# Where VectorE's transform pieces, token combinations and output transpositions stand between two matmul products

## The chip, the cores and the metric

The kernel runs on one core of one Trainium2 chip. The metric is device time in microseconds (us) of one execution. On one core no run can be checked against a second core; the timed runs of both kernels were all classed as fast, and the runs of one kernel agree within 0.3%. One part that varies is the start-up before the first step, 124 to 128 us in the profiled runs. Differences below that are read from the trace of one profiled execution, where a step has a length that repeats to 0.01 us.

## The reference, cut to what matters

```python
# batch, seq, dim = 8, 3008, 256;  d_ff = 2048
X = np.fft.rfft(x, axis=1)                       # along the sequence
y = np.fft.irfft(X * (filt_r + 1j * filt_i), n=seq, axis=1)
h = y.reshape(24064, 256) @ w_in                 # 256 -> 2048
return (h * sigmoid(h)) @ w_out                  # 2048 -> 256
```

The Fourier part is done by matmuls with small tables (stage 1, forward, inverse, stage 3), with additions and multiplications on VectorE between them. The two large products are done by a Strassen-like scheme with seven products in place of eight, which costs extra additions on VectorE.

## The kernel before

All of the time after the start-up is one sequence of 384 steps: 8 batches of 48. A step computes one eighth of the hidden layer of a "pair" (two blocks of 256 or 240 token columns each) and projects the previous step's result. Eight steps make a pair, six pairs a batch. While batch b goes through its 48 steps, the pieces of the transform of batch b+1 are slipped between them. In the timelines VectorE's instructions start in program order (in step 30 the transpositions at 995.67, the token combinations at 996.36, the products at 997.85 and only then the addition behind them at 999.05), so the *place* of a piece in the program decides what it delays.

A step has eight rounds. What VectorE must do in it (lines with `combine(v, ...)`), and when, is set here:

```python
def hidden(step):                                   # ... = cuts
    mm(xo, A11, yt[:, 0, 0:n], True)                # round 0
    nc.scalar.copy(out=sums[:, 0, 0:n], in_=xo)
    yield
    mm(zo, A12, yt[:, 1, 0:n], True)                # round 1
    combine(v, g[:, 0, 0:n], zo, sums[:, 0, 0:n], ALU.add)      # first g<-pyz
    finish()                                        # two g<-g of the step before
    yield
    ...
    mm(yo, S1, t[:, 0, 0:n], True)                  # round 3
    yield
    mm(xo, S3, t[:, 1, 0:n], False)                 # round 4
    nc.scalar.copy(out=sums[:, 2, 0:n], in_=xo)
    combine(v, g[:, 2, 0:n], yo, sums[:, 2, 0:n], ALU.add)      # middle g<-pyz
    ...
    mm(yo, S4, yt[:, 1, n:2 * n], False)            # round 7: overwrites what the middle one read
    combine(v, g[:, 1, 0:n], yo, sums[:, 1, 0:n], ALU.add)      # last g<-pyz
    silu(1)
    combine(v, g[:, 4:6, 0:n], g[:, 1:3, 0:n], g[:, 0:2, 0:n], ALU.subtract)
```

`yo` and `zo` are the two halves of the PSUM tile `pyz`, of which there is one buffer. So product S4 (round 7) waits for the middle addition, and the next step's A12 (round 1) waits for the last one: where they are late, S4 starts 0.47 us after the start of the middle addition (999.05 and 999.52 us, step 30 of the kernel before), A12 0.46 us after that of the last one (935.67 and 936.13 us, behind step 22 of the changed kernel).

The pieces that share VectorE with these, with their times from one start to the next as worked out below:

```python
def multiply(g, k):      # two products of 128x512 out of PSUM: 1.20 us
def add(g, k):           # two sums of 128x256: 0.67 us
def rows(g, i, n=2):     # two sums of 128x512 out of PSUM, then DMAs to d2: 1.32 us
def tokens(pair):        # ty: one 128x512 and two 128x256 differences: 1.49 us
def output(pair, chunk): # two transpositions of 128x256, then 8 DMAs out: 0.69 us
```

Places are given as (step, round); `put` queues a piece, and after each round all that is due is emitted:

```python
def put(step, rnd, piece, *args):
    pending.append((step + rnd / ROUNDS, len(pending), lambda: piece(*args)))
...
for g, step in enumerate((-38, -35, -29, -27, -22, -19)):
    put(at + step, 3, part["forward"], g)
    put(at + step, 5, part["multiply"], g, 0)
    put(at + step + 1, 1, part["multiply"], g, 1)
    put(at + step + 1, 5, part["add"], g, 0)
    put(at + step + 2, 1, part["add"], g, 1)
...
for rnd in range(ROUNDS):
    work = [w for w in work if next(w, work) is not work]   # hidden(step), project(step - 1)
    until(step + rnd / ROUNDS)                              # the pieces due
```

A piece with round 1 to 3 comes to stand behind the first addition and `finish` and ahead of the middle addition: I call this the step's *first interval*. A piece with round 4 to 6 comes between the middle and the last addition: the *second interval*.

## Time and profile before

| | before |
|---|---|
| time, median of 3 (lowest to highest) | 2706.57 us (2706.18 to 2706.76) |
| TensorE busy, weight loads busy | 96%, 80% of the span |
| VectorE, ScalarE, GpSimd busy | 62%, 41%, 17% |
| from the first to the last instruction | 2705.5 us |
| of this ahead of step 0 | 126.6 us |
| one batch of 48 steps (third batch) | 323.1 us |

The table of windows, for the third batch alone (columns: window, its length, then busy time of TensorE, weight loads, VectorE, ScalarE, GpSimd, the granted TensorE clock, DMA share and rate):

```profile
785.40:1108.40 323.00, 320.34 (x2305) 267.91 (x2304) 202.26 (x435) 134.73 (x371) 48.23 (x72) 1.00 0.24 59
```

The granted clock is 1.00 and the DMA share 0.24 in this window, so neither limits the batch as a whole (one step, 36, does wait for a load; it is taken up below). TensorE is shown idle for 2.66 us in the 323 us. The prediction explains why that is only about half of what is lost.

### The profile page before, as it was taken

To read this page: it belongs to the slowest core of one execution; us is meant where nothing else is said; L and a number is where in the kernel's file an instruction comes from. 1 tells how busy PE (TensorE), PEld (TensorE's weight loads), DVE (VectorE), ACT (ScalarE), POOL (GpSimd) and SP (SyncE) were. 2 spreads that over 40 slices of the span, in tenths; PEclk is the share of its full clock that TensorE was granted. 3 is DMA by queue.
4 is the path that set the end of the run, shared out by engine and by line. 5 is a ranking of instruction groups with operands and counts; after the bars stand their busy time and mean duration, and the time that the engine had idled before them with its cause. 6 is when DMAs were issued, how large, how long until landed. Compare 5 with 4: busy or idle time off the path is not lost.

```text
span 2705.5 us, 47315 instructions
## 1 busy us (share of the span) xinstructions
PE 2600.5 (96%) x18432; PEld 2162.2 (80%) x18432; DVE 1675.9 (62%) x3554; ACT 1100.6 (41%) x3000; POOL 448.3 (17%) x653
## 2 busy tenths in 40 slices
PE   4589999999999999999999999999999999999998
PEld 1368888788887888878887888878888788888987
DVE  4886665666566665666656666566665666555554
ACT  1244344443444344444344434444344443444443
POOL 3542111211111111111101111021111111100100
PEclk9599999999999999999999999999999999999999
DMA  9633121421223202331123212132122421110000
GB/s 210 188 101 76 43 49 38 108 61 30 47 66 98 54 24 52 81 86 40 43 53 78 69 56 49 38 98 58 40 49 50 107 53 31 42 34 20 9 16 16
DMA packets 203616, 166.26 MB, mean 61 GB/s; under 512 B 120896, under 2 KB 175808, under 8 KB 203264
## 3 DMA queue, kind: packets, MB, share of 16 engines
q1 hardware_dynamic: 184728, 111.11, 18.3%
q0 software_dynamic: 14992, 47.46, 5.8%
q10 hardware_dynamic: 3672, 4.67, 0.7%
q8 instruction: 145, 2.38, 0.4%
q14 instruction: 79, 0.65, 0.1%
HBM read 88.17 MB, written 74.97 MB: 60 GB/s over the span
## 4 chain that ended last, share of the span: by engine, by line
PE 84%; DVE 9%; DMA 3%; SPq 1%; ACT 1%; issue 1%; POOL 0%; DVEq 0%; ACTq 0%
PE acc L538 37%; PE px L479 22%; PE pyz L479 17%; DVE g L450 3%; PE pd L391 3%; PE pa L292 2%; PE pb L315 2%; PE pc L348 2%; DMA t<-d 1%; DVE q L367 1%; DVE ty L450 1%; DVE p L327 1%; DVE o L568 1%; DVE z L327 1%; DMA x<-in_x_dram 1%
## 5 line engine op out<-in xcount | busy, mean ns | idle before, releaser
L538 PE MATMUL acc<-g,w_t 128*128 128x256 f32 (+1 forms) x5376 | 1513.3, 375 | 0.4 <-DVE g L450 0.4
L538 PEld LDWEIGHTS acc<-g,w_t 128*128 128x128 f32 x5376 | 1022.2, 190 | 116.0 <-DVE g L450 0.8
L450 DVE TENSOR_TENSOR g<-pyz,abc 128x256 f32<-128x256 f32 (+1 forms) x1152 | 478.7, 416 | 590.2 <-ACT abc L500 351.3
L450 DVE TENSOR_TENSOR g<-g 128x256 f32<-128x256 f32 (+3 forms) x1152 | 617.3, 536 | 196.7 <-ACT g L483 183.5
L479 PE MATMUL px<-ty,w_t 128*128 128x256 f32 (+1 forms) x2304 | 690.7, 381 | 4.1 <-ACT abc L494 3.5
L483 ACT ACTIVATE g<-g 128x256 f32<-128x256 f32 (+1 forms) x1152 | 473.3, 411 | 265.6 <-DVE g L450 265.5
L450 POOL TENSOR_TENSOR s<-s 128x256 f32<-128x256 f32 (+1 forms) x329 | 259.2, 805 | 1596.7 <-DVE s L556 1515.2
L479 PEld LDWEIGHTS px<-ty,w_t 128*128 128x128 f32 x2304 | 422.5, 190 | 118.1 <-issue 58.0
L479 PE MATMUL pyz<-y,w_t 128*128 128x256 f32 (+1 forms) x1536 | 461.9, 382 | 18.7 <-DVE g L450 16.9
L479 PEld LDWEIGHTS pyz<-y,w_t 128*128 128x128 f32 x1536 | 278.6, 190 | 83.0 <-DVE g L450 46.7
L494 ACT COPY abc<-px 128x256 f32<-128x256 f32 (+1 forms) x384 | 141.4, 368 | 369.1 <-PE px L479 369.1
L483 ACT ACTIVATE g<-px 128x256 f32<-128x256 f32 (+1 forms) x384 | 146.0, 380 | 300.0 <-PE px L479 300.0
L500 ACT COPY abc<-px 128x256 f32<-128x256 f32 (+1 forms) x384 | 143.2, 373 | 304.8 <-PE px L479 304.6
L479 PE MATMUL px<-y,w_t 128*128 128x256 f32 (+1 forms) x768 | 228.5, 379 | 3.6 <-ACT g L483 2.7
L479 PE MATMUL pyz<-ty,w_t 128*128 128x256 f32 (+1 forms) x768 | 225.4, 375 | 0.7 <-DVE g L450 0.7
L479 PEld LDWEIGHTS px<-y,w_t 128*128 128x128 f32 x768 | 143.1, 190 | 29.2 <-issue 11.1
L479 PEld LDWEIGHTS pyz<-ty,w_t 128*128 128x128 f32 x768 | 145.6, 190 | 18.3 <-DVE g L450 1.8
L487 ACT COPY abc<-px 128x256 f32<-128x256 f32 (+1 forms) x384 | 134.7, 351 | 2.7 <-PE px L479 1.3
L213 DVE COPY y<-pd 128x376 f32<-128x376 f32 x64 | 51.3, 807 | 107.0 <-PE pd L391 107.0
L297 POOL DMA_DIRECT2D d<-t x124 | 64.7, 526 | 294.4 <-ACT abc L500 278.0
L391 PEld LDWEIGHTS pd<-wi_t,t 48*64 48x64 f32 x4096 | 70.7, 140 | 37.6 <-issue 21.9
L315 PE MATMUL pb<-t,d_t 64*32 64x256 f32 x1536 | 62.2, 411 | 38.2 <-DMA t<-d 37.2
(52 smaller groups left out, 1283.8 us busy)
## 6 DMA issues: line engine op xcount, KB each, us to landing
t<-d SPq DMA_DIRECT2D x96, 256.0 KB, 3.9
t<-d SPq DMA_DIRECT2D x128, 192.0 KB, 3.7
d<-t POOLq DMA_DIRECT2D x124, 192.0 KB, 3.0
d<-q POOLq DMA_DIRECT2D x85, 256.0 KB, 2.6
out_dram<-o SPq DMA_DIRECT2D x636, 32.0 KB, 1.8
x<-in_x_dram SPq DMA_DIRECT2D x120, 128.0 KB, 2.9
x<-in_x_dram SPq DMA_DIRECT2D x120, 60.0 KB, 2.8
raw<-in_moe_w_in_dram SPq DMA_DIRECT2D x16, 256.0 KB, 5.9
```

The lines of the kernel that those rows point to most:

```text
L292: nc.tensor.matmul(out=ps[h][64 * par:64 * par + 64], lhsT=wf_t[rows, par], rhs=ut[rows, par], start=True, stop=True)
L297: nc.gpsimd.dma_start(out=d1[par].rearrange("s p n c -> (s p) n c")[:, 4 * u:4 * u + 4, :], in_=t1[64 * par:64 * par + 2 * NS].rearrange(" ...
L315: nc.tensor.matmul(out=ps[k][32 * j:32 * j + 32, ri, :], lhsT=d_t[rows, 4 * g + at, ri, :], rhs=t2[rows, at, :], start=True, stop=True)
L327: nc.vector.tensor_tensor(out=dst, in0=banks[g][k], in1=f_t[m][:, g, k:k + 1, :].to_broadcast([128, 2, C]), op=ALU.mult)
L391: nc.tensor.matmul(out=ps[h][c0:c0 + 64, cb, i, :], lhsT=t4s[g][rows, i, 128 * cb + c0:128 * cb + c0 + 64], rhs=wi_t[rows, :], start=True, ...
L450: eng.tensor_tensor(out=out, in0=in0, in1=in1, op=op)
L479: nc.tensor.matmul(out=out, lhsT=w_t[:, c, 0, jp], rhs=rhs, start=start, stop=True, skip_group_check=True)
L483: nc.scalar.activation(out=g[:, k, 0:n], in_=g[:, k, 0:n] if src is None else src, func=AFT.Silu)
L487: nc.scalar.copy(out=sums[:, 0, 0:n], in_=xo)
L494: nc.scalar.copy(out=sums[:, 1, 0:n], in_=xo)
L500: nc.scalar.copy(out=sums[:, 2, 0:n], in_=xo)
L538: nc.tensor.matmul(out=acc[pair][i][:, h, 0:n], lhsT=w_t[:, c, 1, jp], rhs=g[:, k, 0:n], start=(jp == 0 and h == 0), stop=last, skip_group ...
```

## The change

Its intent: VectorE has room for a piece in each of the two intervals of a step, so each interval should get one large piece or two small ones, in place of two or three large ones in one interval and none in the next. No instruction is added or removed.

```diff
-        for g, step in enumerate((-38, -35, -29, -27, -22, -19)):
-            put(at + step, 3, part["forward"], g)
-            put(at + step, 5, part["multiply"], g, 0)
-            put(at + step + 1, 1, part["multiply"], g, 1)
-            put(at + step + 1, 5, part["add"], g, 0)
-            put(at + step + 2, 1, part["add"], g, 1)
+        for g, places in enumerate((
+                ((-38, 3), (-37, 3), (-37, 5), (-36, 3), (-36, 5)),
+                ((-35, 3), (-35, 5), (-34, 3), (-33, 2), (-33, 5)),
+                ((-29, 3), (-29, 5), (-28, 3), (-28, 5), (-27, 2)),
+                ((-27, 3), (-27, 5), (-26, 3), (-25, 3), (-24, 3)),
+                ((-22, 5), (-21, 3), (-21, 5), (-20, 2), (-20, 5)),
+                ((-20, 3), (-19, 3), (-19, 5), (-18, 3), (-18, 5)))):
+            pieces = (("forward", g), ("multiply", g, 0), ("multiply", g, 1), ("add", g, 0), ("add", g, 1))
+            for (step, rnd), (piece, *args) in zip(places, pieces):
+                put(at + step, rnd, part[piece], *args)
         for g, step in ((0, -32), (2, -24), (4, -16)):
             put(at + step, 7, part["inverse"], g, 2)
             put(at + step, 7, part["even"], g, 0, 2)
             put(at + step + 1, 0, part["even"], g, 1, 2)
-            put(at + step + 1, 3, part["rows"], g, 0, 2)
-            put(at + step + 1, 6, part["rows"], g, 1, 2)
+            put(at + step + 1, 5, part["rows"], g, 0, 2)
+            put(at + step + 2, 3, part["rows"], g, 1, 2)
         put(at - 14, 5, part["load_t4"], 0)
-        for g, (step, rnd) in enumerate(((-12, 3), (-9, 3), (-6, 3), (-3, 3))):
-            put(at + step, rnd, part["stage3"], g)
+        for g, step in enumerate((-11, -9, -6, -3)):
+            put(at + step, 3, part["stage3"], g)
...
-    stores = (((10, 1), (10, 5)), ((19, 5), (20, 1)), ((30, 1), (30, 5)), ((34, 1), (34, 5)),
-              ((42, 1), (42, 5)), ((50, 1), (51, 1)))
+    combines = ((-2, 1), (6, 1), (14, 5), (22, 5), (26, 6), (38, 1))
+    stores = (((10, 1), (10, 5)), ((19, 1), (23, 5)), ((31, 1), (31, 5)), ((35, 1), (35, 5)),
+              ((43, 1), (43, 5)), ((50, 1), (51, 1)))
     for pair in range(len(pairs)):
-        pending.append((NJP * pair - 2 + (5 if pair % per == 3 else 1) / ROUNDS, 100,
-                        lambda pair=pair: tokens(pair)))
+        step, rnd = combines[pair % per]
+        pending.append((pair // per * STEPS + step + rnd / ROUNDS, 98, lambda pair=pair: tokens(pair)))
```

(`at` is 48 times the batch, so -38 is step 10 of the batch before. Cuts are marked.)

## The prediction

> **What bounds the kernel now.** I read the page first: busy shares, the clock row, the chain of waits.
>
> ```profile
> PE 2600.5 (96%) x18432; PEld 2162.2 (80%) x18432; DVE 1675.9 (62%) x3554; ACT 1100.6 (41%) x3000; POOL 448.3 (17%) x653
> ...
> PE 84%; DVE 9%; DMA 3%; SPq 1%; ACT 1%; issue 1%; POOL 0%; DVEq 0%; ACTq 0%
> ```
>
> TensorE sets the pace. VectorE, at 62%, is not saturated, but 9% of the chain runs through it. So I asked for TensorE's own waits:
>
> ```profile
> PE pb L315 <- DMA t<-d: 37.2, 5, 17.3
> PE pyz L479 <- DVE g L450: 17.5, 37, 1.0
> PE pd L391 <- DMA t<-d: 14.7, 9, 7.9
> ```
>
> The first and most of the third lie in the start-up (longest single waits 17.3 and 7.9 us), which the change leaves alone. The second is the target: a product into pyz (the bank pair for yo and zo) waits until VectorE's "g" addition has read that bank. 17.5 us is not its whole price. The timeline of TensorE at the worst place, step 30 of a batch, shows why:
>
> ```profile
> 997.95 0.59 PE L538 MATMUL acc<-g,w_t 128*128 128x256 f32 x2
> 999.52 0.70 PE L479 MATMUL pyz<-y,w_t 128*128 128x256 f32 x2 [0.98 <-DVE g L450]
> ```
>
> Undisturbed pairs follow every 0.43 us and take 0.59; these are 1.57 apart and the second takes 0.70. The loss is 1.57 - 0.43 + 0.10 = 1.24 us though the idle column says 0.98: the modelled tail of the product before hides part, and a refill of 0.10 follows. I therefore measured step lengths instead, from the first px<-y product of one step to that of the next, for all 384 steps. They are remarkably even: 6.04 us with 256 token columns, 5.67 with 240, 5.86 where the width changes; plus 1.22 for a stage-1 (pa) or forward (pb) piece, 2.12 for an inverse pair (pc), 1.28 for a stage-3 piece (pd). A batch of 48 steps should take 317.8 us by this and takes 322.9 to 323.8. The excess, by step of a batch (typical batch; sum over all eight):
>
> step 11: 0.35 (2.45); 14: 0.46 (3.22); 17: 0.15 (1.02); 18: 0.41 (2.88); 20: 0.58 (4.32); 23: 0.83 (5.96); 26: 0.11 (0.86); 30: 1.24 (9.08); 31: 0.36 (2.52); 34: 0.28 (1.93); 36: 0.60 (3.80). Sum 38.0 us.
>
> The last batch has only 0.16 at step 23 and 0.40 at step 30, since no next batch is transformed beside it. Steps 0 to 6 of the first batch lose 13.6 us more to weight rounding; the change does not touch them.
>
> What VectorE does there is in its timeline, an easy step first (27), then step 30:
>
> ```profile
> 975.47 0.88 DVE L450 TENSOR_TENSOR g<-g 128x256 f32<-128x256 f32 x2
> 976.26 0.68 DVE L327 TENSOR_TENSOR z<-pb,filt 128x512 f32<-128x512 f32 x1
> 976.86 0.68 DVE L327 TENSOR_TENSOR p<-pb,filt 128x512 f32<-128x512 f32 x1
> 977.90 0.42 DVE L450 TENSOR_TENSOR g<-pyz,abc 128x256 f32<-128x256 f32 x1 [0.36 <-ACT abc L500]
> 978.25 0.41 DVE L335 TENSOR_TENSOR z<-z,p 128x256 f32<-128x256 f32 x1
> ```
> ```profile
> 994.82 0.88 DVE L450 TENSOR_TENSOR g<-g 128x256 f32<-128x256 f32 x2
> 995.67 0.77 DVE L568 STREAM_TRANSPOSE o<-s 128x256 f32<-128x256 f32 x2
> 996.36 0.65 DVE L450 TENSOR_TENSOR ty<-y 128x512 f32<-128x512 f32 x1
> 997.05 0.88 DVE L450 TENSOR_TENSOR ty<-y,ty 128x256 f32<-128x256 f32 x2
> 997.85 0.68 DVE L327 TENSOR_TENSOR z<-pb,filt 128x512 f32<-128x512 f32 x1
> 998.45 0.68 DVE L327 TENSOR_TENSOR p<-pb,filt 128x512 f32<-128x512 f32 x1
> 999.05 0.42 DVE L450 TENSOR_TENSOR g<-pyz,abc 128x256 f32<-128x256 f32 x1
> ```
>
> In step 27 the middle "g" addition still waits 0.36 us for ScalarE: the piece before it was free. In step 30 three pieces stand before it, it has no idle time, and S4, which overwrites the bank that it reads, comes 0.47 us after its start (999.52).
>
> [...] In step 17, beside GpSimd's additions of the drained sums, the two "g<-g" operations took 0.97 and 0.82 us against 0.40, so the first interval there is short.
>
> **The change part by part.** Nothing is removed or added; I compared the order of instructions on VectorE before and after, step by step. A step has two free intervals on VectorE: the first from its last "g<-g" to the middle addition, the second from there to the addition that closes the step. In the undisturbed timeline, from the step's start, the first is 2.84 to 4.49 us = 1.65 us, the second 4.83 to 6.24 = 1.41 (with 240 columns about 1.5 and 1.31). Overrunning the first costs nothing up to about 0.66 us (S4 starts at 5.62, less 0.47, less 4.49); overrunning the second up to about 0.15 (in the last batch tokens alone overrun by 0.21 and cost 0.06 plus refill).
>
> Pieces, from one start to the next: multiply 1.20 (997.85 to 999.05), row sums 1.32, token combinations 1.49 (996.36 to 997.85), an add 0.67, two transpositions 0.69. Check on step 30: 0.69 + 1.49 + 1.20 = 3.38, 1.73 over 1.65, less 0.66 is 1.07 plus 0.10 refill = 1.17; measured 1.24. So the sizes can be trusted.
>
> - Transposition with multiply in one second interval (steps 10 and 19, 1.89; losses seen in 11 and 20): after, the multiply has the next interval or its own. Steps 11, 27 and 29 then hold a multiply in each interval, 1.20 against 1.65 and 1.41: free. Gain 2.45 + 4.32.
> - Tokens with multiply in the first interval of step 14 (2.69): tokens go to the second alone (240 columns, about 1.44): 0.03 over, free. Gain 3.22.
> - Row sums at steps 17/25/33 move half an interval on, to the second and the next first: 1.32 against 1.31 to 1.41 and 1.5 to 1.65, away from ScalarE's pc copies and the stretched operations. Gain 1.02 + 2.88 + 0.86 + 1.93.
> - Step 22: the add leaves, tokens stay in the second interval of a 240-column step: 1.52 against 1.31, 0.21 over. That is just the last batch's case, which loses 0.16 at step 23. Gain 5.96 less 8 x 0.16 = 4.68.
> - Step 30: transpositions move to 31, the tokens to step 26 behind the forward piece, now placed late there, which lengthens that interval by 1.22; multiplies move to 29. In the last batch tokens alone are 0.1 over, under 0.15. Gain 9.08 + 2.52.
> - Step 36: the stage-3 piece waits for its load, as the SyncE queue is busy with fourteen store issues until 1032.55 and only then issues the load. The stores now stand behind the load and the piece one step later (37). Row sums end 0.6 step later, so the net room grows by over 2 us plus the 6.7 us of stores, against the largest wait of 1.29. Gain 3.80.
>
> Sum: 38.0 - 1.3 = 36.7 us. 2706.6 - 36.7 = 2669.9; I say 2670, a ratio of 1.014.
>
> **The rivals.** (1) *The waits are ScalarE's, not VectorE's.* "DVE g <- ACT abc" is 351 us in the table of waits, far more than 17.5; were it the limit, shifting pieces would give nothing: 2706. Against: this is VectorE's idle time, and where TensorE loses time the addition has none. (2) *A new wait takes the place of the old.* Multiplies and row sums now hold the two rotating transform banks up to half a step longer. The tightest is step 26: row sums end near 4.2 us, the late forward piece needs the bank at 4.74. Should this or the stage-3 loads for step 39 (two steps ahead instead of three, 13 us[...]) fail, 0.3 to 1 us per batch comes back, over seven batches 2 to 7 us each: 2672 to 2684. (3) *Residues.* Intervals filled to 0.01 us (row sums at 17, two multiplies) may spill some tenths: 0.2 us in four places in seven batches is 5.6 us, 2676. (4) *More than the sum.* There is little else to gain: with all 38 us gone it is 2668.5, and 2% would need 54 us.
>
> **Range and chances.** 2670, range 2666 to 2682: the low end allows some of the small unlisted excess, the high end two residues or one new wait. Faster by over 2% (under 2652) 0.01, as it exceeds all the loss; slower by over 2% 0.01; within 2% 0.98.
>
> **What would show it.** Right: step lengths 11 to 36 at their base values, a batch period near 318.0 us, 0.16 us left at step 23 in all eight batches, "PE pyz <- DVE g" falling from 17.5 to about 1, VectorE's busy sum unchanged. Wrong: a forward or inverse product waiting for VectorE "q" or "z" (rival 2), stage 3 at 37 or 39 waiting for its load, or excess at 18, 26 or 34 (rival 3). If the period stays near 323 with other idle reasons, rival 1 held.

## The result, and the profile after

| | before | after |
|---|---|---|
| time, median (lowest to highest, fast runs) | 2706.66 us (2706.18 to 2709.02, 4) | 2669.51 us (2668.88 to 2671.47, 4) |
| ratio | | 0.9862, 95% interval 0.9845 to 0.9879 |
| one batch of 48 steps (third) | 323.1 us | 317.9 us |

Ratios here are the mean time of one kernel's fast runs over that of the other's in the same rounds, so not quite the ratio of the medians. The gain is 1.4%, real but under the 2% that the verdict "faster" asks for; the verdict is "same".

The same views of the changed kernel. The page's busy line and its chain of waits (line numbers are higher by five: L484 is the L479 of before, L455 the L450, L543 the L538):

```profile
PE 2582.3 (97%) x18432; PEld 2165.9 (81%) x18432; DVE 1683.3 (63%) x3554; ACT 1099.8 (41%) x3000; POOL 448.1 (17%) x653
...
PE 93%; DVE 2%; DMA 2%; SPq 1%; issue 1%; ACT 1%; POOL 0%; DVEq 0%; ACTq 0%
```

VectorE has left the chain, 9% to 2%, with the same instructions. Note that TensorE's busy *time* fell by 18 us (2600.5 to 2582.3) with the same 18432 products: part of the loss had been counted as busy.

The waits of TensorE, and the window of one batch:

```profile
PE pyz L484 <- DVE g L455: 2.4, 5, 0.7
```
```profile
776.90:1094.80 317.90, 317.90 (x2306) 268.47 (x2305) 203.53 (x435) 134.72 (x371) 48.25 (x72) 1.00 0.25 60
```

The wait on VectorE's additions fell from 17.5 us in 37 places to 2.4 in 5. The trace puts all five into steps 0 to 5 of the first batch, where the kernel before has 2.2 of its 17.5 us; behind them none is left, and in the third batch TensorE is shown without any idle time. Step 30, the worst before, VectorE first, TensorE at its end below:

```profile
983.77 0.88 DVE L455 TENSOR_TENSOR g<-g 128x256 f32<-128x256 f32 x2
984.57 0.42 DVE L335 TENSOR_TENSOR z<-z,p 128x256 f32<-128x256 f32 x1
984.90 0.42 DVE L336 TENSOR_TENSOR z<-z,p 128x256 f32<-128x256 f32 x1
986.21 0.42 DVE L455 TENSOR_TENSOR g<-pyz,abc 128x256 f32<-128x256 f32 x1 [0.89 <-ACT abc L505]
```
```profile
986.90 0.59 PE L543 MATMUL acc<-g,w_t 128*128 128x256 f32 x2
987.33 0.59 PE L484 MATMUL pyz<-y,w_t 128*128 128x256 f32 x2
```

One small piece stands in the first interval; VectorE then waits 0.89 us for ScalarE's sums, which costs nothing, and S4 follows its predecessor by the usual 0.43 us, at the usual length of 0.59. A releaser with many microseconds in the table of waits, as "DVE g <- ACT abc" (351.3 us before, 321.3 after), is thus here a sign of room on VectorE.

The excess over the base lengths, by step of a batch, summed over the eight batches, is the account on which everything below rests (a step runs from the start of its first px<-y product to that of the next; the base lengths are those of the prediction):

| step | 11 | 14 | 17 | 18 | 20 | 23 | 26 | 30 | 31 | 34 | 36 | sum |
|---|---|---|---|---|---|---|---|---|---|---|---|---|
| before, us | 2.45 | 3.22 | 1.02 | 2.88 | 4.32 | 5.96 | 0.86 | 9.08 | 2.52 | 1.93 | 3.80 | 38.0 |
| after, us | 0 | 0 | 0 | 0 | 0 | 1.28 | 0 | 0 | 0 | 0 | 0 | 1.3 |

No step of the changed kernel outside this list shows more than 0.05 us, apart from the first seven of the first batch, which lose 13.5 us against 13.6 before. VectorE rounds seven weight blocks there (before, five operations of 0.41 to 0.69 us for each, 2.6 us together, from 129.98 to 181.3 us); that they are the cause is the prediction's attribution, and no run tested it. The trace accounts for 36.7 us; the medians differ by 37.2.

### The profile page after: what moved, and what is told of

The parts are those of the page before. It is cut to its first block, busy times and chain, and to the rows that moved or that the text cites. A ratio compares the mean times of both kernels' runs of the same rounds, so it can differ in the third digit from the quotient of the medians.

```text
span 2669.7 us, 47316 instructions
## 1 busy us (share of the span) xinstructions
PE 2582.3 (97%) x18432; PEld 2165.9 (81%) x18432; DVE 1683.3 (63%) x3554; ACT 1099.8 (41%) x3000; POOL 448.1 (17%) x653
## 4 chain that ended last, share of the span: by engine, by line
PE 93%; DVE 2%; DMA 2%; SPq 1%; issue 1%; ACT 1%; POOL 0%; DVEq 0%; ACTq 0%
PE acc L543 42%; PE px L484 25%; PE pyz L484 18%; PE pd L391 3%; PE pa L292 2%; PE pb L315 2%; PE pc L348 2%; SPq L203 1%; DMA x<-in_x_dram 1%; DMA t<-d 1%; DVE g L455 0%; DMA d<-q 0%; DVE u L275 0%; DMA filt<-in_filt_i_dram 0%; DVE q L367 0%
## 5 line engine op out<-in xcount | busy, mean ns | idle before, releaser
L543 PE MATMUL acc<-g,w_t 128*128 128x256 f32 (+1 forms) x5376 | 1513.1, 375 | 0.4 <-DVE g L455 0.4
L543 PEld LDWEIGHTS acc<-g,w_t 128*128 128x128 f32 x5376 | 1022.2, 190 | 116.0 <-DVE g L455 0.8
L455 DVE TENSOR_TENSOR g<-pyz,abc 128x256 f32<-128x256 f32 (+1 forms) x1152 | 479.6, 416 | 553.9 <-ACT abc L505 321.3
L455 DVE TENSOR_TENSOR g<-g 128x256 f32<-128x256 f32 (+3 forms) x1152 | 617.4, 536 | 196.7 <-ACT g L488 183.6
L484 PE MATMUL px<-ty,w_t 128*128 128x256 f32 (+1 forms) x2304 | 690.3, 381 | 4.2 <-ACT abc L499 3.7
L484 PEld LDWEIGHTS px<-ty,w_t 128*128 128x128 f32 x2304 | 422.1, 190 | 118.5 <-issue 58.0
L455 POOL TENSOR_TENSOR s<-s 128x256 f32<-128x256 f32 (+1 forms) x329 | 259.1, 805 | 1318.5 <-DVE s L561 1262.3
L484 PE MATMUL pyz<-y,w_t 128*128 128x256 f32 (+1 forms) x1536 | 455.3, 378 | 1.7 <-DVE g L455 1.7
L484 PEld LDWEIGHTS pyz<-y,w_t 128*128 128x128 f32 x1536 | 283.3, 190 | 45.1 <-DVE g L455 5.6
L484 PE MATMUL px<-y,w_t 128*128 128x256 f32 (+1 forms) x768 | 228.8, 380 | 3.6 <-ACT g L488 2.7
L484 PE MATMUL pyz<-ty,w_t 128*128 128x256 f32 (+1 forms) x768 | 225.4, 375 | 0.7 <-DVE g L455 0.7
L484 PEld LDWEIGHTS px<-y,w_t 128*128 128x128 f32 x768 | 143.3, 190 | 29.2 <-issue 11.1
L484 PEld LDWEIGHTS pyz<-ty,w_t 128*128 128x128 f32 x768 | 145.5, 190 | 18.3 <-DVE g L455 1.8
```

Source lines behind the costliest of these rows:

```text
L455: eng.tensor_tensor(out=out, in0=in0, in1=in1, op=op)
L484: nc.tensor.matmul(out=out, lhsT=w_t[:, c, 0, jp], rhs=rhs, start=start, stop=True, skip_group_check=True)
L543: nc.tensor.matmul(out=acc[pair][i][:, h, 0:n], lhsT=w_t[:, c, 1, jp], rhs=g[:, k, 0:n], start=(jp == 0 and h == 0), stop=last, skip_group ...
```

## The experiments

Theory: TensorE loses time only where what stands in one interval exceeds that interval's room (1.65 us plus 0.66 tolerated in the first, 1.41 plus 0.15 in the second, a little less with 240 columns), and each loss can be worked out from the pieces. These rooms and tolerances are the prediction's estimates, from the starts in an undisturbed step and, for the 0.15, from the loss in the last batch. Rivals: the waits are ScalarE's; it is the load of a step and not its place that counts; later pieces hold buffers and make new waits; the transform's data arrive late for other reasons. All runs gave correct results.

### One part of the change at a time

Three kernels take over one part each. The first, `pieces`, is the kernel before with the new table of places for forward pieces, multiplies and adds, the first hunk of the diff above, and nothing else.

> The kernel before with only the new places of forward pieces, multiplies and adds (row sums, stage 3, tokens, stores as before). If crowded intervals on VectorE are the cause, the excess of each step follows from what stands in it: step 11 to 0; 14, 17, 18, 20, 26, 34, 36 unchanged (0.46, 0.15, 0.41, 0.58, 0.11, 0.28, about 0.6); 23 from 0.83 to 0.16; 30 from 1.24 to about 0.64 (transpositions, tokens and an add: 2.85 us against 2.31); 31 near 0.46. Gain 2.45 + 4.68 + 4.20 - 0.7 = 10.6 us: about 2696. If waits for ScalarE set the pace, nothing moves: 2706.

Measured: 2695.79 us, ratio 0.9960 (0.9945 to 0.9975) to the kernel before. By step: 11 at 0; 14, 17, 18, 20, 26 and 34 unchanged to 0.01 us in a typical batch; 23 at 0.16; 30 at 0.72 where 0.64 was expected; 31 at 0.36 where 0.46 was. Step 36, which the part doesn't touch, showed 3.13 in all instead of 3.80: it hangs on a DMA and varies between runs. The excess fell by 11.1 us. Nothing that ScalarE does was changed, so rival 1 falls.

The second, `tokens_stores`, takes over the last hunk alone (the two lists `combines` and `stores` and the loop that uses them).

> The kernel before with only the new places of token combinations and output transpositions. By the crowding theory: 11, 17, 18, 23, 26, 34 unchanged; 14 to 0 but 15 up to 0.65 (tokens and an add share a second interval, 2.11 us against 1.56); 20, 30, 31, 36 to 0; 27 up to 1.23 (tokens and a multiply in one second interval, 2.69 us). Net gain about 9.8 us: about 2697. If it is transpositions and tokens as such that cost, wherever they stand, nothing moves.

Measured: 2697.41 us, ratio 0.9963 (0.9948 to 0.9977). Steps 14, 20, 30, 31 and 36 went to 0 and 11, 17, 18, 23, 26 and 34 stayed, as expected. The two *new* losses that the sums called for came: 0.62 us at step 15 (0.65 expected), where tokens and an add now share a second interval, and 1.21 at step 27 (1.23 expected), where tokens stand with a multiply. So the same token combination that is free in step 26 of the changed kernel, where it has no multiply beside it and the late forward piece lengthens the interval (step 26 takes 7.26 us there, 1.22 over the 6.04 of a step without a piece), costs 1.2 us here beside a multiply. This part on its own gives back, at steps 15 and 27, 12.8 us of the 22.9 that it saves.

The third, `rows_stage3`:

```diff
-            put(at + step, 3, part["forward"], g)
+            put(at + step, 5 if g == 4 else 3, part["forward"], g)
...
-            put(at + step + 1, 3, part["rows"], g, 0, 2)
-            put(at + step + 1, 6, part["rows"], g, 1, 2)
+            put(at + step + 1, 5, part["rows"], g, 0, 2)
+            put(at + step + 2, 3, part["rows"], g, 1, 2)
...
-        for g, (step, rnd) in enumerate(((-12, 3), (-9, 3), (-6, 3), (-3, 3))):
-            put(at + step, rnd, part["stage3"], g)
+        for g, step in enumerate((-11, -9, -6, -3)):
+            put(at + step, 3, part["stage3"], g)
```

> The kernel before with only row sums half an interval later, stage 3 one step later, and the forward piece of step 26 placed late (its bank is held by the row sums until then). Crowding theory: 17, 18, 26, 34, 36 to 0 (34 may keep 0.05, since row sums and a transposition then share a first interval of 2.3 us), the rest unchanged. Gain 10.5 us: about 2696. Rival (banks held longer make a new wait): forward or stage-3 products wait for VectorE q, excess at 18, 26 or 37.

Measured: 2696.83 us, ratio 0.9963 (0.9950 to 0.9976). Steps 17, 18, 26, 34 and 36 at 0, all others unchanged, no new wait: 10.5 us of excess gone. The three parts alone take away 11.1, 10.1 and 10.5 us, 31.7 together, against 36.7 for the whole. The difference can be told by step: the second part alone makes the new losses of 12.8 us, which the first part clears, while step 30 (3.3 us) and step 36 (3.8, and 0.7 by chance) are counted more than once. So an interval can be relieved by either of two parts, and one part can crowd an interval that another keeps free.

### Why the row sums were late: GpSimd, without moving a piece of VectorE

At steps 17 and 25 the row sums (1.32 us) should fit even their old place. The prediction named two causes at once, the copies of ScalarE that they wait for and the two stretched "g<-g" operations beside GpSimd's additions. `late_sums` tells them apart. It is the kernel before with those additions, for two of six pairs, started later:

```diff
-        for o, a, b in ((2, 0, 2), (5, 0, 5), (3, 5, 3), (6, 3, 6), (0, 5, 1), (4, 0, 4), (1, 3, 1)):
-            combine(eng, s[:, o, 0:n], s[:, a, 0:n], s[:, b, 0:n], ALU.add)
+        def add_up():
+            for o, a, b in ((2, 0, 2), (5, 0, 5), (3, 5, 3), (6, 3, 6), (0, 5, 1), (4, 0, 4), (1, 3, 1)):
+                combine(eng, s[:, o, 0:n], s[:, a, 0:n], s[:, b, 0:n], ALU.add)
+        if pair % per in (1, 2):
+            pending.append((NJP * (pair + 1) + 1 + 4 / ROUNDS, 97, add_up))
+            pending.sort(key=lambda p: p[:2])
+        else:
+            add_up()
```

> The kernel before; only GpSimd's additions of the drained sums of two of six pairs start 1.5 steps after the drain instead of at once, so that they no longer run beside VectorE's operations of steps 17 and 25. Theory: in step 17 (and 25) the two stretched g<-g operations (0.97 and 0.82 us) return to 0.40, the first interval grows by 0.8 us, and the excess of 17, 18 and 26 (0.15, 0.41, 0.11) vanishes without moving a piece of VectorE: gain 4.8 us, about 2702. Rival (the row sums are too long as such, or they wait for ScalarE's copies of the inverse): the excess stays, 2706.6.

The timeline of GpSimd and of VectorE in step 17, before:

```profile
904.30 5.69 POOL L450 TENSOR_TENSOR s<-s 128x256 f32<-128x256 f32 x7 [49.39 <-DVE s L556]
908.45 1.81 DVE L450 TENSOR_TENSOR g<-g 128x240 f32<-128x240 f32 x2
910.18 1.40 DVE L367 TENSOR_TENSOR q<-q,pc 128x512 f32<-128x512 f32 x2
911.50 0.40 DVE L450 TENSOR_TENSOR g<-pyz,abc 128x240 f32<-128x240 f32 x1
```

and with the late sums (the window of this view ends within the additions):

```profile
909.22 0.84 DVE L450 TENSOR_TENSOR g<-g 128x240 f32<-128x240 f32 x2
909.98 1.40 DVE L367 TENSOR_TENSOR q<-q,pc 128x512 f32<-128x512 f32 x2
911.65 0.41 DVE L450 TENSOR_TENSOR g<-pyz,abc 128x240 f32<-128x240 f32 x1 [0.26 <-ACT abc L500]
912.82 3.44 POOL L450 TENSOR_TENSOR s<-s 128x256 f32<-128x256 f32 x4
```

The pair of "g<-g" takes 0.84 us instead of 1.81, the row sums take 1.40 in both, and the middle addition has idle time again. The excess at steps 17, 18 and 26 is gone (0.15, 0.41 and 0.11 per batch before); the kernel took 2701.58 us, ratio 0.9977 (0.9970 to 0.9984; step 36 happened to lose 1.0 us less too). The stretch had not vanished, it had moved: in step 18, where GpSimd now adds, the two operations took 0.62 and 0.82 us, and it cost nothing, because that first interval is empty. A control stands in the same run: the additions beside step 33 were left where they were, its two operations stayed at 0.94 and 0.83 us, and step 34 kept its 0.28. So GpSimd's additions were what made the old place too small. ScalarE's copies, which were not touched, were not needed as a cause. The change got the same 4.8 us by moving the row sums out of the stretched interval.

### The same added work in the first and in the second interval

To test the rooms themselves, the changed kernel got a superfluous repeat of one product of step 27, in seven batches, once ahead of the middle addition (k = 0, `dose_first`) and once behind it (k = 1, `dose_second`). The repeat writes the same value, so the result stays right:

```diff
-            for m, dst in ((0, z), (1, pt)):
+            for m, dst in ((0, z), (1, pt)) + ((1, pt),) * (1 * (b > 0 and g == 4 and k == 0)):
```

> The changed kernel with one superfluous repeat of a product (about 0.7 us with its own wait) in the first interval of step 27, in seven batches. Theory: 1.9 us stand against 1.65 plus the tolerated 0.66: no loss, step 27 and 28 unchanged. Rival (the load of a step counts, not its place): the same loss as with the repeat in the second interval.

> The same repeat in the second interval of step 27: 1.9 us against 1.41 plus 0.15. Theory: 0.34 us and 0.10 of refill at step 28, about 0.44 per batch, 3 us in all. Rival: no loss, as the step's load of 3.1 us is about what both intervals hold together.

VectorE and then TensorE with the repeat in the first interval:

```profile
963.06 1.41 DVE L327 TENSOR_TENSOR p<-pb,filt 128x512 f32<-128x512 f32 x2
964.38 0.41 DVE L455 TENSOR_TENSOR g<-pyz,abc 128x256 f32<-128x256 f32 x1
```
```profile
966.09 0.59 PE L543 MATMUL acc<-g,w_t 128*128 128x256 f32 x2
966.52 0.59 PE L484 MATMUL pyz<-y,w_t 128*128 128x256 f32 x2
```

and in the second:

```profile
968.70 1.41 DVE L327 TENSOR_TENSOR p<-pb,filt 128x512 f32<-128x512 f32 x2
970.02 0.41 DVE L455 TENSOR_TENSOR g<-pyz,abc 128x256 f32<-128x256 f32 x1
```
```profile
969.75 0.59 PE L543 MATMUL acc<-g,w_t 128*128 128x256 f32 x2
970.49 0.48 PE L484 MATMUL pyz<-y,w_t 128*128 128x256 f32 x1 [0.15 <-DVE g L455]
```

The repeat starts 0.73 us after the product that it repeats (1.41 us for the two, 0.68 for one). In the first interval it costs nothing in any step, although the middle addition now follows without idle time. In the second it costs 0.42 us at step 28 in each of the seven batches (0.44 expected), though the profile calls only 0.15 of it idle: the products are 0.74 apart instead of 0.43, and the one behind the wait takes 0.48 instead of 0.38 us. This is the 0.10 that the prediction calls a refill (0.70 instead of 0.59 for the pair in step 30); the traces show its length, not what it consists of. The single times were 2668.84 and 2674.63 us, one run each, so their state is unknown; the step lengths carry the verdict. The load of the step is the same, so it is the place that counts.

With two repeats in the first interval (`dose_first_twice`, the 1 above made 2) its tolerance should be used up:

> The changed kernel with two superfluous repeats in the first interval of step 27 (about 2.6 us against 2.31). Theory: the tolerance is used up: about 0.4 at step 27 and, as the second interval starts late, about 0.3 at step 28; 5 us in seven batches.

Measured: 0.45 at step 27 and 0.23 at step 28 in each of seven batches, 2674.61 us in its one run.

### Step 36: the queue or the place

Step 36 lost its time to a DMA, not to VectorE. The change does two things about it, and two kernels do one each. `stage3_only` is the kernel before with the first stage-3 piece at step 37 (the stage-3 lines of the diff); `stores3_only` leaves stage 3 alone and moves the fourth pair's transpositions:

```diff
-              ((30, 1), (30, 5)), ((34, 1), (34, 5)),
+              ((30, 1), (30, 5)), ((35, 1), (35, 5)),
```

> The kernel before with only the first stage-3 piece one step later (37 instead of 36). Theory: its load, issued once the store issues are through, lands well before; the 3.8 us of waits at step 36 vanish and no wait appears at 37 or 39. Rival: the load for step 39, now two steps ahead, is late, and part comes back there.

> The kernel before with only the transpositions of the fourth pair moved from step 34 to 35, so that their sixteen store issues stand behind the stage-3 load in SyncE's queue. Theory (the queue is the cause): the wait at step 36 vanishes as well, stage 3 staying at 36. Rival (row sums or the landing of their writes are late): about 0.6 stays at 36.

Measured, one run each: 2703.53 and 2702.86 us, beside 2708.14 for the kernel before on the same chip; step 36 (37) at its base length in all batches of both, and all other excesses unchanged. The queue of SyncE, before, and then in `stores3_only`:

```profile
1025.06 7.50 SPq L576 DMA_DIRECT2D out_dram<-o  x16
1032.87 7.16 SPq L377 DMA_DIRECT2D t<-d  x6
```
```profile
1024.05 0.80 SPq L377 DMA_DIRECT2D t<-d  x2
1029.84 8.58 SPq L576 DMA_DIRECT2D out_dram<-o  x16
```

Before, sixteen store issues keep the queue for 7.5 us and the load of stage 3 (t<-d) is issued behind them, 3.7 us ahead of the piece that needs it at 1036.56. With the stores a step later the load goes out at once. The row sums and the landing of their writes were the same in both (the last write landed 10.3 us after the start of step 33), so the queue was the cause. Either half would have done alone.

### The last loss

The one loss left, 0.16 us at step 23, should come from the token combination in the second interval of step 22. `swap22` exchanges it with the multiply of the first:

```diff
-                ((-27, 3), (-27, 5), (-26, 3), (-25, 3), (-24, 3)),
+                ((-27, 3), (-27, 5), (-26, 5), (-25, 3), (-24, 3)),
...
-    combines = ((-2, 1), (6, 1), (14, 5), (22, 5), (26, 6), (38, 1))
+    combines = ((-2, 1), (6, 1), (14, 5), (22, 1), (26, 6), (38, 1))
```

It ran on the same chip as the changed kernel once more (`after_again`).

> The changed kernel once more, as the yardstick for the next run on the same chip: about 2670, excess only at step 23 (0.16 in each of the eight batches).

> The changed kernel with tokens and multiply of step 22 exchanged: tokens (1.52 us) in the first interval, which tolerates about 0.66 us of overrun, the multiply (1.20) in the second, which holds 1.31. Theory: the 0.16 us at step 23 goes in all eight batches, 1.3 us in all, and nothing comes instead: about 2668.3 when the changed kernel shows 2669.6. Rival (two large pieces in one step cost, in whatever order): 0.16 stays or grows.

In the changed kernel the last addition of step 22 starts at 935.67 and the next step's A12 is late:

```profile
935.67 0.40 DVE L455 TENSOR_TENSOR g<-pyz,abc 128x240 f32<-128x240 f32 x1
935.67 0.57 PE L543 MATMUL acc<-g,w_t 128*128 128x240 f32 x2
936.13 0.67 PE L484 MATMUL pyz<-y,w_t 128*128 128x240 f32 x2
```

In `swap22`, VectorE and TensorE at the same place:

```profile
932.50 0.68 DVE L327 TENSOR_TENSOR z<-pb,filt 128x512 f32<-128x512 f32 x1
933.10 0.68 DVE L327 TENSOR_TENSOR p<-pb,filt 128x512 f32<-128x512 f32 x1
933.80 0.41 DVE L455 TENSOR_TENSOR g<-pyz,abc 128x240 f32<-128x240 f32 x1
```
```profile
934.00 0.57 PE L543 MATMUL acc<-g,w_t 128*128 128x240 f32 x2
934.41 0.57 PE L484 MATMUL pyz<-y,w_t 128*128 128x240 f32 x2
```

The products are 0.41 us apart instead of 0.46 and the second pair takes 0.57 us instead of 0.67; step 23 is at its base length in all eight batches, where `after_again` has its 0.16 in all eight. The times are 2668.81 us (2667.33 to 2672.33, four runs; ratio 0.9857, 0.9840 to 0.9873) against 2670.71 (2668.97 to 2671.97; ratio 0.9861, 0.9846 to 0.9876): the right direction, but 1.3 us is within what the runs differ by, so only the step lengths show this gain.

## Why the prediction was right

- *What bounds the kernel.* TensorE, with its losses at pyz behind VectorE's additions: shown by the fall of that wait from 17.5 to 2.4 us and of VectorE's share of the chain from 9% to 2%. The foreseen value of about 1 us was missed: it left out the 2.2 us in steps 0 to 5 of the first batch, which the prediction itself says the change does not touch, while the 0.16 us at step 23 shows in no wait of the table.
- *The size of the loss from step lengths, 38.0 us, and not from the idle column.* Right: 36.7 us of it went, though the idle column could have promised only 17.5 for that wait. This step carried the forecast.
- *Crowding step by step.* Every line came out: steps 11, 14, 17, 18, 20, 26, 30, 31, 34 and 36 went to base length, and the 0.16 at step 23 stayed in all eight batches. That 0.16 was read from the last batch, and the tolerance of 0.15 fitted to it, so step 23 is no test of the sums. The partial kernels and the doses are: the losses worked out for them, from 0.3 to 1.23 us per batch, were met within 0.1 us.
- *Row sums at 17 and 25.* The gain was right and the working named two causes; `late_sums` shows that GpSimd's additions alone were enough.
- *Step 36.* Right; but the two reliefs were added together, and each is enough alone. One reading was wrong without effect: the queue held sixteen store issues for 7.5 us and not fourteen for 6.7, since the view had been cut at 1026 us.
- *Rivals.* The new wait at step 26, the stage-3 load for step 39 and the residues of a tenth here or there did not come: step 26 takes 7.26 to 7.27 us and step 39 7.32 in each of the first seven batches, their base lengths, and the 128 stage-3 loads landed 3.6 us after their issue in the median, 7.1 at most. These rivals were the reason for the long upper end of the range; the measured 2669.51 lies 0.5 us below the point forecast.
- *Side forecasts.* "VectorE's busy sum unchanged" was wrong by a little: 1683.3 us against 1675.9. The two traces show why: operations that follow each other closely overlap by some 0.08 us (in step 30 the 128x512 products, of 0.68 us each, start 0.60 apart; in step 27 the 128x256 sums, of 0.41 and 0.42 us, 0.33 apart), which the busy time counts once. These overlaps fell from 143.0 to 137.7 us in all, and the operations themselves took 2.1 us longer (1818.9 and 1821.0 us, overlaps counted twice).

The forecast is exact to a degree that a reader should not expect: the start-up alone varies by some 4 us between the profiled runs, more than the difference.

## What to carry to other kernels

When an engine that is far from saturated (here VectorE, busy for 62% of the span) delays the one that sets the pace, draw up the room between its fixed obligations and what stands in each gap: the same added product cost 0.42 us in one gap and nothing in the other, at the same load. Measure the loss by the length of repeating units rather than by the idle column, which showed 0.98 of 1.24 us in one place and 0.15 of 0.42 in another. And move pieces together: a third of the change alone created new crowds that another third had been meant to clear.
